# A planned schedule with one v fetch per batch, traced landing times, and the last strided outputs transposed by transfer

## The chip, the cores and the metric

The kernel runs on one core of a Trainium2 chip. The core has a matrix engine (TensorE, "PE"), a vector engine (VectorE, "DVE"), a scalar engine (ScalarE, "ACT"), a general engine (GpSimd, "POOL"), a queue engine that only issues transfers (SyncE, "SP"), and 16 transfer engines that carry what GpSimd and SyncE issue. TensorE reads from the on-chip memory SBUF and writes into eight banks of PSUM, which ScalarE and VectorE empty. The metric is the time of one execution on the device in microseconds (us), the median of several runs.

## The reference

Attention over 8 batches, 8 heads, 576 positions of 64 numbers each, and then a two-layer feed-forward part over the 4608 tokens. The first four heads see the last 32 positions ("local"); the last four see every 32nd position back ("strided").

```python
scores = scale * np.matmul(q, k.transpose(0, 1, 3, 2))
mask_local = (rel >= 0) & (rel < 32)
mask_strided = (rel >= 0) & (pos[None, :] % 32 == pos[:, None] % 32)
scores = np.where(masks, scores, -1e9)          # local for heads 0-3, strided for 4-7
attn = softmax(scores)
x = np.matmul(attn, v)                          # to (4608 tokens, 512)
h = x @ w_in                                    # 512 -> 2048
r = np.maximum(h, 0.0)
g = s * (r * r) + b
out = g @ w_out                                 # 2048 -> 512
```

The inputs are 32-bit, and so is the output; the kernel works in 16-bit floats, and GpSimd's transfers convert on the way in.

## The kernel before

The kernel is one long program without loops on the chip. While it is built, a planner with a clock of its own decides in which order the instructions of each engine stand. Nothing on the chip waits for that clock: the chip runs each engine's instructions in the order given, and each waits for its own inputs. A planned duration or landing time therefore moves instructions and costs nothing itself.

The planner knows three engines ("A", "V", "P" for ScalarE, VectorE, GpSimd) and three kinds of transfers issued by SyncE: "D", transposes within SBUF, "X", stores of x to a scratch in DRAM, and "Y", transposes back from there. LAT is the time from the end of the issue to the landing, in ns.

```python
class Plan:
    LAT = {"A": 70.0, "V": 70.0, "P": 70.0, "D": 12000.0, "X": 7000.0, "Y": 12000.0}
    ...
            eng = min(p[1], key=lambda e: max(self.free[e], r) + p[1][e])
            end = max(self.free[eng], r, self.t - self.SLACK) + p[1][eng]
            ...
                self.done[k] = end + (6000.0 if soon else p[4] or self.LAT[eng])
```

The loads of v. The local half is put in SBUF as bands of 96 positions, 32 partitions up, with a column of ones beside each 64 numbers; the strided half comes whole for batches 0 to 3 ("vs", then cast) and head by head later.

```python
    def v_band(b, h):
        return v[b, h].rearrange("(t p) d -> p t d", p=LQ)          # 96 rows of 6 x 64
    ...
    def load_vl(b):
        vl = v_loc[b % NV]
        for h in range(4):
            nc.gpsimd.dma_start(out=vl[LPAD:128, h, :, 0:D], in_=v_band(b, h))

    def load_vs(b):
        vs = v_str[b % NV]
        for h in range(4):
            nc.gpsimd.dma_start(out=vs[:, h, :, 0:D],
                                in_=v[b, 4 + h].rearrange("(p j) d -> p j d", j=ST))
```

The planned landings of what GpSimd fetches: one ring in which each transfer comes after the one before.

```python
    def landing(cost):
        nonlocal ring
        ring = max(ring, plan.t + 2000.0) + cost
        return ring + (6000.0 if plan.t > 60000.0 else 600.0)

    def weights_in(eng):                # after batch 0's loads
        ...
        load_w_in()                     # three parts: 512, 512, 1024 columns
        ring = 15300.0
        for keys, cost in ([0], 2700), ([1], 2500), ([2, 3], 5000): ...

    def second(eng):                    # batch 1, then w_out in four parts
        fetch_qk(1)
        load_vl(1)
        plan.done["raw", "vl", 1] = landing(3200)
        ...
        early_v(1)
        weights_out(range(4))           # landing(2400 if c < 3 else 3000)
```

The attention output x of one pair of heads becomes the transposed input xT of the feed-forward part in one of two ways: by TensorE against the identity, through PSUM, and a copy; or by transfer. The strided outputs by transfer go out to DRAM and come back transposed.

```python
        x_by_dma = b >= 2 if loc else XS_DMA <= b < B - 1      # XS_DMA = 4
        ...
        def xtrans(j, group):           # one transpose on TensorE (line 662)
            ...
                nc.tensor.matmul(out=st["px"][:, nq * j:nq * j + nq], lhsT=st["x"][:, j, :],
                                 rhs=ident[0:nq, 0:nq], is_transpose=True)
        def x_out(eng):                 # line 685
            nc.sync.dma_start(out=x_dram[2 * (b % 2) + mm].rearrange("(p j) d -> p j d", j=nt),
                              in_=st["x"])
        def x_in(eng):                  # line 689
            nc.sync.dma_start_transpose(out=x_slot(m, b), in_=x_dram[2 * (b % 2) + mm])
```

TensorE's main lines are: 429 and 437 the transposes of q and k, 557 the scores, 614 attention times v, 662 the transposes of x, 907 the first feed-forward matmul, in nine blocks of 512 tokens, 965 and 875 the second, and 1201 matmuls without use in the first 21 us.

```python
        # 907: needs the four xT pieces of the block's tokens and a part of w_in
        needs.append(("w_in", ft // 4))
        # 965: needs a piece of g and a quarter of w_out
        s = Step(f, 216, needs=[("g", T, ft), ("w_out", ft // 4)], ...)
```

## Time and profile before

| | before |
|---|---|
| time, median of 3 runs | 305.05 us (304.64 to 305.45) |
| span of the profiled execution | 304.4 us |
| TensorE, instructions of matmul kind | 2674 |
| GpSimd busy | 99.3 us, 33% |
| transfers: GpSimd's queue, SyncE's queue | 18.08 MB in 57232 packets; 18.78 MB in 43562 |
| v band fetches, each 72 KB | 28, 8.5 us from issue to landing (median) |
| ScalarE waiting for the first feed-forward matmul | 69.9 us, in 74 waits |

A line of the waits reads: engine, tile and line that waited, what ended the wait, the total in us, the number of waits, the longest. In a timeline the columns are the start in us, the length, the engine, the line, the operation with what it writes and reads, the number of like instructions merged, and in brackets the idle time of the engine before it with what ended it. Matmuls overlap: the recorded length of one is longer than the distance from its start to the next start.

### The profile page before, as it was taken

The page shows a single profiled execution, that of the slowest core. Times are in us where ns is not written, and L with a number is a line of the kernel's source. Part 1 is how long each engine was busy: PE and PEld are TensorE (multiplying, and loading weights), DVE is VectorE, ACT ScalarE, POOL GpSimd, SP SyncE. Part 2 cuts the span into 40 slices and gives each one's busy share as a digit, 9 for nine tenths or more (in the row PEclk, how much of TensorE's full clock was granted, in tenths as well). Part 3 has the DMA queues.
Part 4 walks back from the last instruction along what each step waited for, and adds up shares of the span by engine and source line. Part 5 has one row for each costly group of instructions (what it writes and reads, how often), then busy time and mean ns, then how long its engine had stood idle before and what let it go on. Part 6 is the DMA issues. An engine that isn't in the chain of part 4 may idle for free.

```text
span 304.4 us, 6800 instructions
## 1 busy us (share of the span) xinstructions
PE 296.4 (97%) x2674; PEld 205.8 (68%) x2674; DVE 216.6 (71%) x474; ACT 183.9 (60%) x330; POOL 99.3 (33%) x146
## 2 busy tenths in 40 slices
PE   8998999999999999999999999999999999999995
PEld 3764655666555568767567776778888666766784
DVE  6665897698966688737997698777765366737563
ACT  2966963898747677478585946695725445445300
POOL 8771753930961095029502961200000000000000
PEclk9999999999999999999999999999999999999999
DMA  8999999999999699999999999944010200300123
GB/s 136 183 201 202 137 213 190 179 198 149 83 160 165 98 100 149 132 186 147 142 153 172 142 160 159 155 105 131 14 37 34 72 34 0 106 0 2 69 82 126
DMA packets 100826, 37.29 MB, mean 122 GB/s; under 512 B 80907, under 2 KB 97803, under 8 KB 100795
## 3 DMA queue, kind: packets, MB, share of 16 engines
q0 software_dynamic: 57232, 18.08, 60.1%
q1 hardware_dynamic: 43562, 18.78, 33.3%
q8 instruction: 21, 0.34, 0.5%
q14 instruction: 11, 0.08, 0.1%
HBM read 36.86 MB, written 10.32 MB: 155 GB/s over the span
## 4 chain that ended last, share of the span: by engine, by line
PE 83%; DMA 8%; DVE 3%; POOL 3%; issue 1%; ACT 1%; POOLq 0%
PE ps_f L907 36%; PE ps_f L875 20%; PE ps_f L965 12%; DMA kl<-in_k_dram 5%; PE ps_s L557 3%; PE ps_a L614 3%; DMA vs<-in_v_dram 2%; PE ps_s L875 2%; DMA xT<-x_dram 1%; PE ps_t L875 1%; PE ps_s L965 1%; PE ps_t L614 1%; PE ps_t L662 1%; PE ps_t L437 1%; PE ps_f L437 1%
## 5 line engine op out<-in xcount | busy, mean ns | idle before, releaser
L907 PE MATMUL ps_f<-xT,w_in_sb 128*128 128x512 f16 (+4 forms) x696 | 148.1, 340 | 0.0
L934 ACT ACTIVATE u<-ps_f 128x512 f16<-128x512 f32 x137 | 80.8, 595 | 72.6 <-PE ps_f L907 69.9
L907 PEld LDWEIGHTS <-w_in_sb 128*128 128x128 f16 x704 | 71.7, 113 | 33.1 <-DMA w_in_sb<-in_moe_w_in_dram 0.5
L875 PEld LDWEIGHTS <-gT 128*128 128x128 f16 x512 | 49.0, 98 | 12.5 <-issue 0.4
L965 PE MATMUL ps_f<-w_out_sb,gT 128*128 128x512 f16 x176 | 47.6, 379 | 0.0
L875 PE MATMUL ps_f<-w_out_sb,gT 128*128 128x256 f16 x312 | 44.2, 273 | 0.3 <-DVE o L806 0.3
L944 DVE TENSOR_TENSOR gT<-u 128x1024 f16<-128x1024 f16 x46 | 32.1, 697 | 15.1 <-ACT u L934 14.4
L942 ACT ACTIVATE gT<-u 128x1024 f16<-128x1024 f16 x26 | 27.5, 1057 | 0.7
L640 DVE TENSOR_TENSOR x_nat<-ps_a,rec 72x256 f16<-72x256 f32 (+1 forms) x55 | 25.3, 459 | 0.9
L316 POOL DMA_DIRECT2D v_loc<-in_v_dram x28 | 20.7, 759 | 14.3 <-DMA w_in_sb<-in_moe_w_in_dram 6.0
L965 PEld LDWEIGHTS <-gT 128*128 128x128 f16 x192 | 17.0, 98 | 11.1
L575 ACT ACTIVATE p_str<-ps_s 72x432 f16<-72x432 f32 (+1 forms) x45 | 20.1, 481 | 4.7 <-PE ps_s L557 4.6
L575 ACT ACTIVATE p_loc<-ps_s 128x384 f16<-128x384 f32 x46 | 20.8, 494 | 2.2 <-PE ps_s L557 1.8
L614 PEld LDWEIGHTS <-p_str 72*128 72x128 f16 x256 | 15.3, 98 | 7.3 <-issue 0.4
L747 DVE TENSOR_TENSOR gT<-gT 128x1024 f16<-128x1024 f16 x28 | 18.5, 683 | 1.4 <-ACT gT L942 1.3
L875 PE MATMUL ps_f<-w_mix,gT 128*128 128x256 f16 x144 | 19.3, 273 | 0.0
L875 PEld LDWEIGHTS <-S 128*128 128x128 f16 x160 | 15.5, 98 | 3.7
L629 DVE RECIPROCAL rec<-ps_a 72x4 f32<-72x4 f32 (+1 forms) x55 | 9.7, 177 | 11.2 <-PE ps_a L614 11.0
L321 POOL DMA_DIRECT2D v_str<-in_v_dram x16 | 13.0, 816 | 9.6 <-PE ps_f L907 5.6
L583 DVE TENSOR_TENSOR p_loc<-p_loc,masks 128x1152 f16<-128x1152 f16 x14 | 10.5, 750 | 7.6 <-ACT p_loc L575 7.4
L875 PE MATMUL ps_f<-w_mix,S 128*128 128x256 f16 x96 | 13.4, 273 | 0.0
L976 DVE SCALAR_TENSOR_TENSOR o<-ps_f,s_sb,bcs 128x512 f32<-128x512 f32 x11 | 8.2, 749 | 6.4 <-PE ps_f L965 6.2
(162 smaller groups left out, 413.2 us busy)
## 6 DMA issues: line engine op xcount, KB each, us to landing
out_dram<-o SPq DMA_DIRECT2D x34, 256.0 KB, 3.4
w_out_sb<-in_moe_w_out_dram POOLq DMA_DIRECT2D x4, 512.0 KB, 9.4
v_loc<-in_v_dram POOLq DMA_DIRECT2D x28, 72.0 KB, 8.5
qs<-in_q_dram POOLq DMA_DIRECT2D x6, 288.0 KB, 6.6
ks<-in_k_dram POOLq DMA_DIRECT2D x6, 288.0 KB, 8.0
ql<-in_q_dram POOLq DMA_DIRECT2D x5, 288.0 KB, 9.7
kl<-in_k_dram POOLq DMA_DIRECT2D x16, 72.0 KB, 3.8
v_str<-in_v_dram POOLq DMA_DIRECT2D x16, 72.0 KB, 9.9
```

Of the source, the lines that this page charges most:

```text
L316: nc.gpsimd.dma_start(out=vl[LPAD:128, h, :, 0:D], in_=v_band(b, h))
L321: nc.gpsimd.dma_start(out=vs[:, h, :, 0:D], in_=v[b, 4 + h].rearrange("(p j) d -> p j d", j=ST))
L575: nc.scalar.activation(out=st["pw", g][0:nk, 0:2 * n * nq], in_=st["s", g][0:nk, 0:2 * n * nq], func=AF.Exp, scale=scale)
L614: nc.tensor.matmul(out=st["a"][:, j % per, :], lhsT=st["pw", g][0:nk, i * nq:i * nq + WIDE], rhs=vt[0:nk, 2 * mm + e, j, :])
L640: nc.vector.tensor_tensor(out=st["x"][:, j0:j0 + per, 64 * e:64 * e + 64], in0=st["pa", e, j][0:nq, 0:per, 0:D], in1=st["rec", e, j][0:nq, ...
L747: nc.vector.tensor_tensor(out=at(out), in0=at(x), in1=at(y), op=op)
L875: nc.tensor.matmul(out=gts[name, T, t][:, 0] if halves else gts[name, T][:, t], lhsT=lhs(k, t), rhs=rhs(k), start=fresh and k == 0 and (ha ...
L907: nc.tensor.matmul(out=gts["h", T, ft][:, lo:hi], lhsT=w_in_sb[min(ft // 4, 2)][:, ct].rearrange("p (c x l) -> p c l x", x=128, l=4)[:, ma ...
L934: nc.scalar.activation(out=u, in_=gts["h", T, ft], func=AF.Relu)
L942: nc.scalar.activation(out=g, in_=u, func=AF.Square)
L944: nc.vector.tensor_tensor(out=g, in0=u, in1=u, op=ALU.mult)
L965: nc.tensor.matmul(out=gts[id_], lhsT=gts[T][:, ft, ts * 128:(ts + 1) * 128], rhs=w_out_sb[:, ft, cols], start=(ft == 0), stop=(ft == NFT ...
```

## The change

Three things are changed. The local band of v of a batch is fetched in one transfer of 96 partitions by 24 runs of 64 numbers, instead of four of 6 runs. The planner's landing times are set to what a trace showed: of the transposes and stores (LAT), of the ring's tail after 60 us of the planner's clock, and of each early fetch. And the strided outputs of the last batch go by transfer like those of batches 4 to 6, instead of over TensorE. The aim is an order in which no engine stands before an input that has not landed, and less work on TensorE.

```diff
--- before.py
+++ after.py
@@ -21,7 +21,7 @@
 
 
 
-    LAT = {"A": 70.0, "V": 70.0, "P": 70.0, "D": 12000.0, "X": 7000.0, "Y": 12000.0}
+    LAT = {"A": 70.0, "V": 70.0, "P": 70.0, "D": 10000.0, "X": 6500.0, "Y": 6000.0}
 
     SLACK = 800.0
     LATER = {"g": 1500.0, "S": 1500.0, "in": 2500.0, "w_mix": 2500.0}
@@ -311,9 +311,9 @@
             nc.gpsimd.dma_start(out=h4(dst)[r], in_=view_s(src, b)[r])
 
     def load_vl(b):
-        vl = v_loc[b % NV]
-        for h in range(4):
-            nc.gpsimd.dma_start(out=vl[LPAD:128, h, :, 0:D], in_=v_band(b, h))
+        nc.gpsimd.dma_start(
+            out=v_loc[b % NV].rearrange("p h t d -> p (h t) d")[LPAD:128, :, 0:D],
+            in_=v.rearrange("b h (t p) d -> b p (h t) d", p=LQ)[b, :, 0:4 * LT])
 
     def load_vs(b):
         vs = v_str[b % NV]
@@ -475,7 +475,7 @@
 
         k_by_dma = b >= (KB_DMA if loc else 3)
         q_by_dma = b >= (QB_DMA if loc else QS_DMA)
-        x_by_dma = b >= 2 if loc else XS_DMA <= b < B - 1
+        x_by_dma = b >= 2 if loc else XS_DMA <= b
 
         def k_dma(eng):
             if loc:
@@ -1024,7 +1024,7 @@
         nonlocal ring
         ring = max(ring, plan.t + 2000.0) + cost
 
-        return ring + (6000.0 if plan.t > 60000.0 else 600.0)
+        return ring + (3500.0 if plan.t > 60000.0 else 600.0)
 
     def both(name, b):
         return [("in", name, b, mm) for mm in range(2)]
@@ -1041,13 +1041,13 @@
                 arrive(both(name + "l", b), landing(4600))
                 continue
             if b < HEAD_T:
-                arrive(both(name + "l", b), landing(1500))
+                arrive(both(name + "l", b), landing(2400 if name == "q" else 2600))
                 continue
-            plan.done["raw", name, b] = landing(1700 if b > 1 else 1450)
+            plan.done["raw", name, b] = landing(1700 if b > 1 else 2400 if name == "q" else 2500)
             for mm in range(2):
                 pair_post(b, name, mm, ("raw", name, b))
         for name in ("qs", "ks"):
-            arrive(both(name, b), landing(2000 if b > 1 else 1750))
+            arrive(both(name, b), landing(2000 if b > 1 else 1200))
 
     def fetch_v(b):
         load_vl(b)
@@ -1064,7 +1064,7 @@
 
         loaded[b, "vs"] = inp.tile([SQ, NS], FP16, tag="vs", name="vs")
         load_s(loaded[b, "vs"], v, b)
-        plan.done["raw", "v", False, b] = landing(1800)
+        plan.done["raw", "v", False, b] = landing(1800 if b > 1 else 1300)
         for mm in range(2):
             cast_v(b, False, mm, ("raw", "v", False, b))
 
@@ -1113,13 +1113,13 @@
 
         fetch_qk(1)
         load_vl(1)
-        plan.done["raw", "vl", 1] = landing(3200)
+        plan.done["raw", "vl", 1] = landing(2000)
         for mm in range(2):
             rows_before(1, mm, ("raw", "vl", 1))
         early_v(1)
         weights_out(range(4))
 
-    plan.post(both("vl", 0) + both("vs", 0) + [("w",)], {"P": 14000.0}, second, [("free",)])
+    plan.post(both("vl", 0) + both("vs", 0) + [("w",)], {"P": 12500.0}, second, [("free",)])
 
     att = []
     left = {}
@@ -1146,7 +1146,7 @@
                         {"P": 2900.0 + (2200.0 if b + 2 >= QB_DMA else 0.0)},
                         lambda eng, b=b: fetch_qk(b + 2), [("fetch", b + 2)])
                 last_av.after = when_all("av", b, lambda b=b: plan.post(
-                    [("fetch", b + 2)] + both("vs", b), {"P": 3600.0}, lambda eng: fetch_v(b + 2),
+                    [("fetch", b + 2)] + both("vs", b), {"P": 3600.0 if b >= 2 else 1500.0}, lambda eng: fetch_v(b + 2),
                     [("fetch_v", b + 2)]))
 
     f1, f2 = [], []
```

## The prediction

> **What bounds the kernel now.** I read the page's busy times and slices first, then the list of what TensorE waited for, then TensorE's and GpSimd's timelines over the one stretch where those waits lie. Busy times and slices (40 equal slices of 7.6 us, tenths):
>
> ```profile
> PE 296.4 (97%) x2674; PEld 205.8 (68%) x2674; DVE 216.6 (71%) x474; ACT 183.9 (60%) x330; POOL 99.3 (33%) x146
> ...
> PE   8998999999999999999999999999999999999995
> ...
> DMA  8999999999999699999999999944010200300123
> ```
>
> TensorE is full from the fourth slice to the last. The transfer engines are full for the first 26 slices, but TensorE hardly notices after the start. All of its waits (total us, times, longest):
>
> ```profile
> PE ps_t L429 <- DMA ql<-in_q_dram: 1.4, 1, 1.4
> ...
> PE ps_t L429 <- DMA kl<-in_k_dram: 0.6, 1, 0.6
> ...
> PE ps_f L875 <- DVE o L806: 0.3, 1, 0.3
> PE ps_a L614 <- DVE x_nat L640: 0.2, 1, 0.2
> ```
>
> (The three lines left out are in the first 19 us, which the change does not touch.) Where the first two lie, TensorE's timeline: start, length, line, operands, idle before it.
>
> ```profile
> 23.00 4.05 PE L907 MATMUL ps_f<-xT,w_in_sb 128*128 128x512 f16 x18
> 28.49 0.45 PE L429 MATMUL ps_t<-ident,ql 96*64 96x96 f16 x12 [1.44 <-DMA ql<-in_q_dram]
> 28.77 0.42 PE L429 MATMUL ps_f<-ident,ql 96*64 96x96 f16 x12
> 29.12 1.49 PE L907 MATMUL ps_f<-xT,w_in_sb 128*128 128x512 f16 x6
> 31.23 0.45 PE L429 MATMUL ps_t<-ident,kl 96*64 96x96 f16 x12 [0.62 <-DMA kl<-in_k_dram]
> ```
>
> Eighteen 512-column matmuls in 4.05 us, the last recorded as 0.38, are 216 ns from start to start. Then TensorE stands still for batch 1's q and k, with other work at hand: the third part of w_in had landed by 26.9, as GpSimd's timeline of the same stretch shows.
>
> ```profile
> 22.06 0.75 POOL L316 DMA_DIRECT2D v_loc<-in_v_dram  x1 [1.96 <-DMA w_in_sb<-in_moe_w_in_dram]
> 26.89 0.72 POOL L316 DMA_DIRECT2D v_loc<-in_v_dram  x1 [4.08 <-DMA w_in_sb<-in_moe_w_in_dram]
> 28.73 0.73 POOL L316 DMA_DIRECT2D v_loc<-in_v_dram  x1 [1.11 <-DMA ql<-in_q_dram]
> 31.47 0.72 POOL L316 DMA_DIRECT2D v_loc<-in_v_dram  x1 [2.01 <-DMA kl<-in_k_dram]
> 32.31 1.18 POOL L311 DMA_DIRECT2D vs<-in_v_dram  x2
> 33.63 2.15 POOL L334 DMA_DIRECT2D w_out_sb<-in_moe_w_out_dram  x4
> ```
>
> Each v band waits for the transfer issued eight places before it: GpSimd's transfers in this trace count on eight semaphores in turn. So the four bands go out over 10 us, the last at 31.5, and the queue nearly runs dry behind them. The transfer view of 33 to 36 us, in slices of 75 ns:
>
> ```profile
> GB/s 96 111 111 121 120 126 108 84 82 72 36 50 65 65 92 77 38 34 10 38 79 79 118 145 68 123 150 177 191 177 164 218 191 164 178 177 191 150 191 260
> ```
>
> From 33.5 to 35 it moves some 60 GB/s where the band ran at 120 just before and w_out runs at 180 after.
>
> [...] matmuls recorded as 379 ns start every 216. [...] the bands take 0.75 us on GpSimd and land 3.9 to 14.9 us after issue. [...] w_out's 128 rows take 554 ns to issue, a band's 576 rows 752.
>
> **Part 1, v in one transfer.** Seven batches by three fewer issues are 21 off GpSimd. From the two issue times, (752-554)/(576-128) = 0.44 ns per row; one issue of 2304 rows is then about 1.5 us, an estimate, against 4 x 0.75 = 3.0. That is 7 x 1.5 = 10 us off an engine that is 33% busy: worth nothing by itself. Rows and bytes stay the same, so a full queue gains nothing either. What it can gain is the hole: the whole band would go out at 22.1, the strided v at 26.9 and 28.7 and w_out from about 31.3, each again behind the eighth before it. 1.5 us at 60 instead of 120 GB/s is about 0.8 us, so w_out's first quarter, which by the trace's completion events landed at 40.2, should land near 39.4.
>
> **Part 2, the order of early work.** The built instruction order shows the same TensorE sequence up to the last of the 18 matmuls, then five 512-column matmuls before the q transposes where there were none, and eight between those and the k transposes where there were six.
> - Before q: 5 x 0.216 = 1.08 us of the gap filled. Gap from the 18th matmul's slot end (26.9) to 28.49 was 1.6; 0.5 stays.
> - Before k: 2 x 0.216 = 0.43 filled; of 0.8 [...] 0.4 stays. Together 1.5 us gained by 31.3.
> - Given back 1: the new order puts the first scores right behind qs, at 31.23 plus two sets of 12 k transposes at 22 ns, one matmul and eight at 32 ns = 32.2. In the old trace the k copy to SBUF ended at 32.35. About 0.2 lost.
> - Given back 2: summing start-to-start spacings (216 ns for 512 columns, 82 for 192, 63 for 144, 33 for 65, 32 for 72) along the new order, the first w_out matmul falls at 38.8, with the 0.2 at 39.0, where the old one ran at 40.8. It then waits for w_out until 39.4: 0.4 lost. If part 1 moves no landing it waits until 40.2 and loses 1.2, which is most of the gain. So the two parts hang together.
> - The wait before an attention matmul at 41.8, 0.4 of lost start time: in the new order the multiply that frees its bank stands further ahead. Counted as 0.4 gained.
>
> Part 2 nets 1.5 - 0.2 - 0.4 + 0.4 = 1.3 us.
>
> **Part 3, the last strided outputs.** Sixteen transposes of 72 columns leave TensorE, 104 to 88 of this kind:
>
> ```profile
> L662 PE MATMUL ps_t<-ident,x_nat 72*128 72x72 f16 x72 | 5.1, 196 | 0.0
> ...
> xT<-x_dram SPq DMA_TRANSPOSE x6, 3.3
> ```
>
> Recorded 196 ns each, they start every 32, so 16 x 32 ns = 0.5 us, and it counts, since TensorE is the bound there (215 to 219 us). Two copies also leave PSUM. The way round through DRAM costs two stores and two transposes, 3.3 us to land, with the last strided values ready by 219 and block 7, which reads them, starting at 237.0. It is hidden.
>
> **Part 4, shorter planned latencies.** They run nothing faster; they let consumers stand earlier. From block 2 on the attention steps stand some 8 to 10 us earlier in TensorE's order against the feed-forward blocks. That removes perhaps half of the single later loss (0.47 us before 177.4, behind a full VectorE): 0.25. The danger is an order that trusts a landing too much. Traced issue-to-landing of the in-SBUF transposes is 2.6 to 10.6 us, so at most 9.3 after the 1.3 us of issue, under the 10 now planned; of the DRAM ones 2.7 to 4.8, under 6. I charge 0.3 for a new wait.
>
> Sum: 1.3 + 0.5 + 0.25 - 0.3 = 1.75; the full sum of spacings along both orders from 39.1 and 43.1 on differs by 2.3 at the end, before the charge. I take 2.1: 305.05 - 2.1 = 302.9.
>
> **Rivals.** (a) The w_out landing takes the wait's place and nothing is kept of part 2: 0.5 to 1.0 gained in all, 304.3. For it: the queue is full, first in, first out, and the bytes are the same. Against it: the hole above. (b) The new order stalls in the middle, where three engines were in balance; the earlier attention crowds ScalarE and VectorE (more squares go to ScalarE, 26 to 31): 304 to 307. For it: landings of 10.6 us in crowded stretches; against: none of these waits showed before, and planned latencies were far above the traced ones. (c) The one large issue blocks GpSimd or the ring, w_out comes later, 305 to 306. For: 2304 rows at once was never run here; against: some 1,850 rows were already outstanding at 22 us (w_in 512, ql and kl 384 each, qs and ks 288 each).
>
> **Range and chances.** TensorE has about 3.5 us to give at most: the waits after 19 us (1.6, 0.8, 0.4, 0.47) and the transposes, so below 301.5 is not reachable, and the 2% line at 298.9 is out of reach. Slower by 2%, 311.2, would need new waits of 8 us. 8 in 10: 301.8 to 304.8. Chances 0.01 faster, 0.97 same, 0.02 slower.
>
> **What would show it.** Right: the waits for ql and kl near 0.5 and 0.4; w_out in flight by 34 us with no dip before it; the first L965 matmul near 39.4; block 7 about 2 us earlier; L662 at 88. Wrong: L965 waiting for w_out by over 1 us (part 1), or any single TensorE wait above 0.5 us after 60 us (part 4).

## The result and the profile after

| | before | after |
|---|---|---|
| time, median of 4 runs each, on one chip | 304.85 us (304.5 to 305.45) | 313.95 us (312.82 to 318.16) |
| ratio | | 1.0293, 95% interval 1.0258 to 1.0328 |
| span of the profiled execution | 304.4 us | 315.6 us |
| TensorE, instructions of matmul kind | 2674 | 2658 |
| ScalarE and VectorE waiting with a copy for a v band | none | 10.3 us in 3 waits and 8.4 us in 2 |

The change costs 2.9%. The prediction was 302.9, with 304.8 as the upper end of its range. The profiled execution of after is the longest of its executions (318.16), so its losses are larger than those of the median. The other executions on record span 310.4 to 312.1 us at mean clocks of 0.993 to 1.000, so by an estimate from the lowest of these clocks, (1 - 0.993) x 311.3, at most 2.2 us of theirs are due to the clock; none of them has a trace.

The page of after, busy times and slices (40 slices of 7.9 us, tenths; the third row is the granted clock of TensorE):

```profile
PE 299.9 (95%) x2658; PEld 206.9 (66%) x2658; DVE 213.8 (68%) x472; ACT 188.6 (60%) x334; POOL 85.8 (27%) x121
...
PE   7999989999999999999959994999999999999995
PEclk9999999999999999999979999899999999999999
DMA  8999999997999799999999999923500200200223
```

TensorE has two holes that it did not have before, in slices 21 and 25 (a 5 and a 4). The clock row shows less than nine tenths in slice 21 itself and in slice 26. What TensorE waited for, in the list of its waits:

```profile
PE ps_f L907 <- ACT u L934: 7.8, 2, 4.1
...
PE ps_a L429 <- DMA kl<-in_k_dram: 0.5, 1, 0.5
```

The first line is nearly everything: two waits, 7.8 us, by the first feed-forward matmul for a free PSUM bank, which ScalarE (line 934, the eviction to u) had not emptied. The kl wait is in the first batch's loads at the very start (7.5 us); batch 1's ql and kl waits, which the change was aimed at, are gone. TensorE's timeline at both places:

```profile
155.86 0.82 PE L875 MATMUL ps_f<-w_out_sb,gT 128*128 128x256 f16 x6
156.52 1.03 PE L907 MATMUL ps_f<-xT,w_in_sb 128*128 128x512 f16 x4
161.30 1.02 PE L907 MATMUL ps_f<-xT,w_in_sb 128*128 128x512 f16 x4 [3.75 <-ACT u L934]
...
191.23 0.82 PE L875 MATMUL ps_f<-w_out_sb,gT 128*128 128x256 f16 x6
196.14 1.53 PE L907 MATMUL ps_f<-xT,w_in_sb 128*128 128x512 f16 x4 [4.09 <-ACT u L934]
```

Why was ScalarE late? Its own timeline around the two places:

```profile
155.39 0.58 ACT L934 ACTIVATE u<-ps_f 128x512 f16<-128x512 f32 x1
160.04 0.73 ACT L338 COPY v_loc<-v_loc 32x640 f16<-32x640 f16 x1 [4.07 <-DMA v_loc<-in_v_dram]
160.67 1.05 ACT L934 ACTIVATE u<-ps_f 128x512 f16<-128x512 f32 x2
...
194.88 0.73 ACT L338 COPY v_loc<-v_loc 32x640 f16<-32x640 f16 x1 [5.16 <-DMA v_loc<-in_v_dram]
195.51 1.05 ACT L934 ACTIVATE u<-ps_f 128x512 f16<-128x512 f32 x2
```

A small copy (line 338: it puts the last 32 rows of one part of the v band under the next part) stood in ScalarE's order at a place where the band had not landed. ScalarE stood idle before it for 4.07 and 5.16 us, and the evictions behind it start only at 160.67 and 195.51. The waits of TensorE, 3.75 and 4.09 us, are put down to these evictions and end at 161.30 and 196.14. The copy itself takes 0.7 us and TensorE does not need it at that moment. VectorE stood before the twin of this copy at the same time, for 2.97 and 5.43 us until 160.04 and 194.88, so neither of the two engines that empty the banks did so meanwhile. The two bands are those of batches 6 and 7, counted from 0: GpSimd fetches seven, for batches 1 to 7, and these are the last two. (The quoted expectations call them those of batches 5 and 6.) The chain that ended last runs the same way (start, length, what):

```profile
141.69 18.33 DMA v_loc<-in_v_dram
160.04 0.73 ACT v_loc L338
160.76 0.49 ACT u L934
161.30 1.04 PE ps_f L907 x4
...
178.00 16.86 DMA v_loc<-in_v_dram
```

The bands took 18.3 and 16.9 us from issue to landing. What the two holes cost, from the table of busy times by stretch, for after (each hole, and the stretch behind it in which the trace has the clock at half; stretch, sum, then busy time and instructions of PE, weight loads, VectorE, ScalarE, GpSimd, then the mean granted clock, the transfer share, GB/s):

```profile
157.00:161.30 4.30, 0.55 (x4) 0.18 (x3) 1.30 (x4) 1.26 (x3) 0.00 (x0) 1.00 1.61 175
162.39:165.80 3.41, 3.41 (x19) 2.47 (x17) 1.17 (x3) 1.66 (x4) 0.00 (x0) 0.50 1.40 163
191.50:196.20 4.70, 0.61 (x7) 0.42 (x5) 1.02 (x2) 1.32 (x3) 0.00 (x0) 1.00 1.51 167
196.52:199.93 3.41, 3.41 (x10) 1.36 (x9) 2.49 (x4) 0.73 (x3) 0.00 (x0) 0.50 1.65 163
```

Start time lost in the holes, counted from where the next matmul would have started: 3.9 + 4.3 = 8.2 us. Lost to the lower clock, an estimate from the two stretches at 0.50: 2 x 3.41 x (1 - 0.50) = 3.4. Together 11.6 us, against a span longer by 315.6 - 304.4 = 11.2. So the loss of the profiled execution is all here, and whatever else the change moved comes to about -0.4.

The blocks of the first feed-forward layer say the same: the last matmul of block 0 starts 1.3 us earlier than before (39.15 against 40.41), that of block 4 6.8 us later (180.35 against 173.59), that of block 5 12.4 us later (216.28 against 203.92), and from the start of block 6 to the last matmul of block 8 after is 1.2 us shorter (74.29 against 75.51).

### The profile page after: what moved, and what is told of

Same layout as the page of the kernel before. It is cut to its first block, busy times and chain, and to the rows that moved or that the text cites. A ratio compares the mean times of both kernels' runs of the same rounds, so it can differ in the third digit from the quotient of the medians.

```text
span 315.6 us, 6716 instructions
## 1 busy us (share of the span) xinstructions
PE 299.9 (95%) x2658; PEld 206.9 (66%) x2658; DVE 213.8 (68%) x472; ACT 188.6 (60%) x334; POOL 85.8 (27%) x121
## 4 chain that ended last, share of the span: by engine, by line
PE 65%; DMA 21%; POOL 6%; issue 3%; DVE 2%; ACT 1%; SPq 1%; POOLq 0%; DVEq 0%
PE ps_f L907 28%; PE ps_f L875 16%; DMA v_loc<-in_v_dram 11%; PE ps_f L965 9%; DMA vs<-in_v_dram 5%; DMA ql<-in_q_dram 3%; PE ps_s L557 3%; PE ps_a L614 2%; DMA kT<-ks 2%; POOL ql L293 2%; PE ps_s L875 2%; PE ps_t L875 1%; PE ps_s L965 1%; POOL kl L293 1%; PE ps_t L437 1%
## 5 line engine op out<-in xcount | busy, mean ns | idle before, releaser
L907 PE MATMUL ps_f<-xT,w_in_sb 128*128 128x512 f16 (+4 forms) x696 | 150.5, 343 | 7.8 <-ACT u L934 7.8
L907 PEld LDWEIGHTS <-w_in_sb 128*128 128x128 f16 x704 | 72.6, 114 | 41.8 <-issue 9.4
L875 PEld LDWEIGHTS <-gT 128*128 128x128 f16 x512 | 49.5, 99 | 12.7 <-issue 0.6
L965 PE MATMUL ps_f<-w_out_sb,gT 128*128 128x512 f16 x176 | 48.3, 379 | 0.2
L944 DVE TENSOR_TENSOR gT<-u 128x1024 f16<-128x1024 f16 x41 | 28.1, 685 | 19.4 <-ACT u L934 18.9
L942 ACT ACTIVATE gT<-u 128x1024 f16<-128x1024 f16 x31 | 32.8, 1057 | 1.5 <-DVE u L936 0.6
L965 PEld LDWEIGHTS <-gT 128*128 128x128 f16 x192 | 17.1, 98 | 12.2 <-issue 1.0
L747 DVE TENSOR_TENSOR gT<-gT 128x1024 f16<-128x1024 f16 x28 | 18.5, 682 | 2.0 <-ACT gT L942 1.8
L1036 POOL COPY gate<-kT 1x1 f16<-1x1 f16 x6 | 2.1, 354 | 47.7 <-DMA kT<-ks 47.7
L614 PEld LDWEIGHTS <-p_loc 128*128 128x128 f16 x192 | 9.3, 98 | 5.1 <-DVE p_loc L583 0.9
## 6 DMA issues: line engine op xcount, KB each, us to landing
ks<-in_k_dram POOLq DMA_DIRECT2D x6, 288.0 KB, 10.3
```

The source lines that it names most:

```text
L614: nc.tensor.matmul(out=st["a"][:, j % per, :], lhsT=st["pw", g][0:nk, i * nq:i * nq + WIDE], rhs=vt[0:nk, 2 * mm + e, j, :])
L747: nc.vector.tensor_tensor(out=at(out), in0=at(x), in1=at(y), op=op)
L875: nc.tensor.matmul(out=gts[name, T, t][:, 0] if halves else gts[name, T][:, t], lhsT=lhs(k, t), rhs=rhs(k), start=fresh and k == 0 and (ha ...
L907: nc.tensor.matmul(out=gts["h", T, ft][:, lo:hi], lhsT=w_in_sb[min(ft // 4, 2)][:, ct].rearrange("p (c x l) -> p c l x", x=128, l=4)[:, ma ...
L942: nc.scalar.activation(out=g, in_=u, func=AF.Square)
L944: nc.vector.tensor_tensor(out=g, in0=u, in1=u, op=ALU.mult)
```

## The experiments

All ratios below are against the kernel before, run beside it on the same chip, with 95% intervals. They leave out executions more than 1.5% above the kernel's fastest, which hides part of a loss that comes and goes: of the 20 executions of the tail alone (306.11 to 315.26 us) six are left out, and the median of all 20 is 1.0% above before, where its ratio says 0.65%. Waits of TensorE that are given without a line are lost start time, from where the next matmul would have started; a line's brackets hold the idle time, which is up to 0.4 us less. The names of theories are those in the quoted expectations. "Early" stands for the landings and issue times of batch 1 and of the early v fetch, "tail" for the ring's 6.0 or 3.5 us after 60 us, "LAT" for the line of latencies, "last x" for the last batch's strided outputs by transfer.

### Each part alone

**One v transfer, all else as before.** The order on TensorE, ScalarE and VectorE is that of before.

```diff
-        for h in range(4):
-            nc.gpsimd.dma_start(out=vl[LPAD:128, h, :, 0:D], in_=v_band(b, h))
+        nc.gpsimd.dma_start(
+            out=v_loc[b % NV].rearrange("p h t d -> p (h t) d")[LPAD:128, :, 0:D],
+            in_=v.rearrange("b h (t p) d -> b p (h t) d", p=LQ)[b, :, 0:4 * LT])
```

> The kernel before with only the v band fetched in one transfer; the order on TensorE, ScalarE, VectorE and SyncE is that of before, instruction for instruction. Theory A (a late landing and an early copy are both needed): the band lands some 16 to 18 us after its issue instead of 8 to 10, for batch 5 near 160.5, but the copies that read it stand at 161.4 in this order, so no wait above 1 us: 304.3 to 305.5 us. Rival B (the single transfer does it alone): ScalarE and VectorE wait for the band for 3 us or more in one or two batches: 308 us or more.

308.73 us (306.58 to 311.25), ratio 1.0088 (1.0059 to 1.0117). GpSimd's timeline of this kernel at batch 6's band

```profile
145.71 1.20 POOL L314 DMA_DIRECT2D v_loc<-in_v_dram  x1
```

and ScalarE's:

```profile
161.98 1.35 ACT L338 COPY v_loc<-v_loc 32x640 f16<-32x640 f16 x2
```

The band lands at 160.4, 14.7 us after its issue; in before the four went out at 142.6 to 144.8 and the last landed at 154.8, 12.2 us after the first issue. For batch 7 it is 14.9 against 10.4 us. The copies stand late enough not to wait (161.98), but the 6.6 us of room that before had are down to 1.6. The span of the profiled execution is 305.2 and holds no wait above 1 us after 60 us. Some of the loss lies outside the span: time minus span is 2.25 us here and 1.8 in before. The rest comes and goes between executions, which spread over 4.7 us: five of the ten have mean clocks of 0.989 to 0.994, and none of these has a trace. Neither theory holds as it stands: no wait, as A had it, but the time that B wanted. Why the single transfer costs 0.9% is not shown.

**The early landings alone, the tail alone, LAT alone, last x alone.**

```diff
# early_alone: the hunks of fetch_qk, fetch_v, early_v, second and the last one
-            plan.done["raw", name, b] = landing(1700 if b > 1 else 1450)
+            plan.done["raw", name, b] = landing(1700 if b > 1 else 2400 if name == "q" else 2500)
# ...
# tail_alone
-        return ring + (6000.0 if plan.t > 60000.0 else 600.0)
+        return ring + (3500.0 if plan.t > 60000.0 else 600.0)
# lat_alone
-    LAT = {"A": 70.0, "V": 70.0, "P": 70.0, "D": 12000.0, "X": 7000.0, "Y": 12000.0}
+    LAT = {"A": 70.0, "V": 70.0, "P": 70.0, "D": 10000.0, "X": 6500.0, "Y": 6000.0}
# last_x_alone
-        x_by_dma = b >= 2 if loc else XS_DMA <= b < B - 1
+        x_by_dma = b >= 2 if loc else XS_DMA <= b
```

> The kernel before with only the landings of the first two batches, of w_in's and w_out's time and the two early planned issue costs changed; v in four transfers, tail and latencies of before. Theory E (the early part is sound; what costs is that attention was moved ahead from batch 2 on): the waits for ql and kl fall as in the changed kernel, a wait of up to 1.2 us for w_out appears, nothing waits above 0.5 us after 60 us; 303.5 to 305 us. Rival F (the early order upsets the later one): 306 us or more.

305.86 us, ratio 0.9990 (0.9971 to 1.0009). The ql and kl waits are gone; in their place TensorE waits 0.91 us for w_out at 38.4, which lands at 39.3. In time nothing is gained, where 303.5 to 305 were expected (before had 305.84 beside it).

> The kernel before with only the planned tail of GpSimd's fetches at 3.5 us instead of 6.0; v in four transfers. Of 704 first-layer and the second-layer matmuls, 436 stand ahead of the first use of batch 5's v band, against 471 before and 427 in the changed kernel. Theory E: the tail alone moves attention ahead, SyncE's transposes fall over GpSimd's fetches, v and k land later than their consumers stand, and TensorE waits 1 to 4 us in batches 5 and 6: 308 to 313 us. Rival D (it takes the shorter latencies of SyncE's transposes as well): 304.5 to 306.5 us.

308.89 us, ratio 1.0065 (1.0036 to 1.0094). New waits of 2.65 us at 187.6, for a q piece that VectorE lays out, and 1.71 at 190.6. VectorE's timeline of this kernel shows what the q piece stood behind:

```profile
189.22 0.32 DVE L338 COPY v_loc<-v_loc 32x640 f16<-32x640 f16 x1 [3.52 <-DMA v_loc<-in_v_dram]
189.56 1.28 DVE L338 COPY qD_loc<-qTl 64x576 f16<-64x576 f16 x4
```

and TensorE's:

```profile
190.24 0.49 PE L557 MATMUL ps_s<-qD_loc,kT_alt 128*128 128x192 f16 x4 [2.48 <-DVE qD_loc L338]
```

So the short tail alone, with four v transfers, already puts copies of batch 7's band ahead of its landing (VectorE waits 6.4 us in two), and the same blocking passes on to TensorE. That band's last quarter lands at 189.1, 18.5 us after the first issue.

> The kernel before with only the planned latencies of SyncE's transposes and stores shortened (10.0, 6.5 and 6.0 us); v in four transfers, tail 6.0. 451 matmuls of the two layers stand ahead of batch 5's v band. Theory E: half of the shift of the changed kernel, so smaller waits: 305 to 308 us. Rival D: these latencies are the main cause: 309 us or more.

307.05 us, ratio 1.0036 (1.0011 to 1.0060). New waits after 60 us: 1.61 us at 196.7, for a transposed k piece, and 1.0 at 203.3, for a mask. The traced execution is the longest of the twenty (311.09).

> The kernel before with only the last batch's strided outputs transposed by transfer; all planned latencies and the four v transfers as before. Sixteen TensorE transposes fewer, 32 ns each from start to start: 0.5 us less, 305.2 to 305.5 beside a before of about 305.8. Rival H: the two stores and two transposes added between 200 and 215 us fall over other transfers and something waits: 306 us or more.

307.17 us, ratio 1.0036 (1.0014 to 1.0058): sixteen matmuls fewer, and slower. TensorE's timeline of this kernel:

```profile
237.90 1.47 PE L875 MATMUL ps_f<-w_out_sb,gT 128*128 128x256 f16 x12 [0.84 <-DVE Va L794]
239.20 1.89 PE L907 MATMUL ps_f<-xT,w_in_sb 128*128 128x512 f16 x8
```

Block 7 starts at 239.2 instead of 237.0. The planner believed that the transposed pieces come back 12 us after issue ("Y"), so it kept block 7 back and put second-layer matmuls there, which then waited for their banks. So the time is rival H's, by another cause.

None of the five parts alone has a ratio above 1.009, and the sum of their losses is 2.2%, less than the 2.9% of all together.

### Taking parts back out of after

**Four v transfers again, in after's order.**

```diff
-        nc.gpsimd.dma_start(out=v_loc[b % NV].rearrange(...)[LPAD:128, :, 0:D], ...)
+        for h in range(4):
+            nc.gpsimd.dma_start(out=vl[LPAD:128, h, :, 0:D], in_=v_band(b, h))
```

> The changed kernel with only the v band fetched in four transfers again; the order on TensorE, ScalarE, VectorE and SyncE is that of the changed kernel. Theory A: each last quarter lands 10 to 12 us after its issue, near 154 for batch 5, before its copies at about 156; no wait of TensorE above 1 us after 60 us, 302 to 304 us. Rival C (the earlier order fills the queues so that v comes late however it is fetched): the quarters of batch 5 land at 158 or later and the waits of about 4 us stay: 309 us or more.

312.78 us, ratio 1.0239 (1.0211 to 1.0268). Most of the loss stays, so it is not the single transfer that makes it. ScalarE's timeline of this kernel at batch 6's copies

```profile
155.72 0.73 ACT L338 COPY v_loc<-v_loc 32x640 f16<-32x640 f16 x1
```

VectorE's:

```profile
159.75 0.32 DVE L338 COPY v_loc<-v_loc 32x640 f16<-32x640 f16 x1 [3.02 <-DMA v_loc<-in_v_dram]
```

and TensorE's:

```profile
160.91 0.49 PE L875 MATMUL ps_f<-w_out_sb,gT 128*128 128x256 f16 x3 [2.78 <-DVE Va L794]
```

With quarters each copy waits for its own two. ScalarE's finds them landed; VectorE's stands 3.0 us before the last one, at 159.7. The four had gone out at 141.1 to 143.3, 1.5 us earlier than in before, and landed up to 4.9 us later: 152.7 to 159.7 against 151.1 to 154.8. So the order alone, with the same transfers, delays the landing. The v copies are not all of it: of TensorE's late waits here as much goes to transposed k pieces that land late, 1.7 us at 166.7 and 1.5 at 198.7:

```profile
168.41 0.57 PE L557 MATMUL ps_s<-qD_str,kT 128*72 128x144 f16 x6 [1.56 <-DMA kT<-ks]
```

**The old tail in after.**

```diff
-        return ring + (3500.0 if plan.t > 60000.0 else 600.0)
+        return ring + (6000.0 if plan.t > 60000.0 else 600.0)
```

> The changed kernel with only the planned tail of GpSimd's fetches after 60 us at 6.0 us again instead of 3.5. Theory A: the copies of the v band's rows stand 2.5 us or more later, the band still lands 15 to 18 us after issue; the waits of ScalarE for the band fall from 10.3 us in all to under 3, 302.5 to 305 us. Rival B (the single transfer is late whatever is planned): waits of 3 us or more stay, 308 us or more. Rival D (the shorter latencies of SyncE's transposes are the cause, not the tail): waits stay as they are, 312 to 314 us.

308.72 us, ratio 1.0098 (1.0060 to 1.0137). One planning number gives two thirds of the loss back; the 302.5 to 305 that theory A expected are missed by what is left, about the cost of the single transfer. VectorE's timeline of this kernel at batch 6:

```profile
165.54 0.57 DVE L338 COPY v_loc<-v_loc 32x640 f16<-32x640 f16 x2
```

The band lands at 163.1, 17 us after its issue at 146.1, as slowly as in after; but the copies stand at 165.5 and do not wait. No wait after 60 us is above 0.73.

**The copies of v alone later in after.** Only the planned landing of the band is raised by 6 us; q and k keep after's numbers.

```diff
-            plan.done["raw", "vl", b] = landing(4600)
+            plan.done["raw", "vl", b] = landing(4600) + 6000.0
```

> The changed kernel with only the planned landing of the v band 6 us later from batch 2 on, so that the copies of its rows stand later on ScalarE and VectorE. Theory A (these copies block the engines in order, and with them the evictions that TensorE waits for): no wait for the band above 1 us, 302 to 304.5 us. Rival C (v is late for the attention itself, or the queues are clogged): TensorE waits as long at another place, 309 us or more.

311.04 us, ratio 1.0183 (1.0138 to 1.0229), where theory A expected 302 to 304.5. The v waits are gone, but others have come up. From TensorE's timeline of this kernel:

```profile
195.77 0.37 PE L614 MATMUL ps_a<-v_loc,p_loc 128*128 128x65 f16 x6 [0.56 <-DVE p_loc L583]
...
198.21 0.57 PE L557 MATMUL ps_s<-qD_str,kT 128*72 128x144 f16 x6 [1.45 <-DMA kT<-ks]
```

Now the scores wait for transposed k pieces (their weight loads 2.7 us in 2 waits), and the attention matmuls for the masks. Moving the copies of v back thus gives 1.1 of the 2.9 per cent; in what stays, TensorE waits for other landings that the same tail makes the planner expect early. That these waits are the whole rest is not shown.

**Old LAT in after.**

```diff
-    LAT = {"A": 70.0, "V": 70.0, "P": 70.0, "D": 10000.0, "X": 6500.0, "Y": 6000.0}
+    LAT = {"A": 70.0, "V": 70.0, "P": 70.0, "D": 12000.0, "X": 7000.0, "Y": 12000.0}
```

> The changed kernel with only the latencies of SyncE's transposes and stores as before; tail 3.5, v in one transfer. 435 matmuls of the two layers stand ahead of batch 5's v band, against 427 in the changed kernel, 463 with only the tail restored, 471 before. Theory E (the further ahead attention stands, the longer the waits): between the 308.7 of the kernel with only the tail restored and the 314 of the changed one, 310 to 313 us. Rival D (these latencies are the main cause): 308 us or less.

320.00 us (316.58 to 320.73), ratio 1.0441 (1.0405 to 1.0477). The expectation was missed: with longer planned latencies it is the slowest kernel of all. It has the same two waits as after (3.85 at 157.9 and 4.49 at 192.0), and a clock row that is lower behind them:

```profile
PE   8999989999999999999969994999999999999995
PEclk9999999999999999999969997899999999999999
```

Behind each wait this trace has the clock at half for 6.83 us, twice as long as in after (160.61 to 167.44 and 194.74 to 201.57; the mean clock is 0.55 from 162 to 168 and 0.67 from 192 to 200), so by the same estimate up to 6.8 us are lost to it instead of 3.4 (for the first 1.1 and 1.7 us of the two TensorE still stood). The mean clocks of its six executions, 0.979 to 0.989, amount to 3.5 to 6.7 us lost, against 0 to 2.2 in the untraced ones of after. So by this estimate the clock can account for most of what it loses beyond after, 1.5% or about 4.5 us. Why its clock stays low for longer is not shown.

**Both numbers back, one v transfer; and both parts without any of the planned latencies.**

```diff
# late_plan_one_v: after, with tail 6000.0 and the old LAT
# early_and_last_x: before, with the early landings and last x (four v transfers)
```

> The changed kernel with both the planned tail and the latencies of SyncE's transposes as before; so the kernel above with v in one transfer, and the same order of TensorE, ScalarE, VectorE and SyncE as that one. Theory E: no more than the cost of the single transfer is left, about 2.7 us as in the run of that part alone: 307 to 308.5 us, no wait of 4 us. Rival B (the single transfer is the main cause): 310 us or more.

310.49 us, ratio 1.0154 (1.0120 to 1.0188); waits of 1.80 us at 197.3 and 1.00 at 239.8. The 307 to 308.5 expected are missed; the time is in rival B's range.

> The kernel before with the two parts kept that did no harm: the early landings and the last strided outputs by transfer. Four v transfers, tail 6.0, latencies of before; 471 matmuls of the two layers stand ahead of batch 5's v band, as before. Theory E: the early part gives 0.3 and the transposes 0.5 us; 304.5 to 305.3 beside a before of about 305.8, no TensorE wait above 0.5 us after 60 us. Rival: the gains do not add, 305.5 or more.

306.83 us, ratio 1.0032 (1.0013 to 1.0050); waits of 1.50 us for w_out at 39.0 (landed at 40.4) and 1.01 at 237.5. Here too the gain expected (304.5 to 305.3) did not come. The two kernels have the same order and differ in the v transfers alone: 1.2%.

**Four v transfers with the old tail, or with the old LAT.**

```diff
# four_v_tail_back: after, four v transfers, tail 6000.0
# four_v_lat_back: after, four v transfers, the old LAT (tail 3500.0)
```

> The changed kernel with v in four transfers and the tail at 6.0 us; the shorter latencies of SyncE's transposes, the early landings and the last strided outputs by transfer stay. Theory K (without the shortened tail nothing large is lost; the transfer and the latencies only make it worse): 0.998 to 1.004 of before, no wait above 1 us after 60 us. Rival D (the shorter latencies do it alone): 1.010 or more.

306.84 us, ratio 1.0026 (1.0005 to 1.0048). No late wait, as theory K expected; w_out is waited for 1.97 us at 39.3, since it landed at 41.3.

> The changed kernel with v in four transfers and the latencies of SyncE's transposes as before; the tail stays at 3.5 us. Theory K: the shortened tail costs by itself as in the run of that part alone and the four transfers land soon enough: 1.005 to 1.015 of before, against 1.044 with one transfer. Rival (the tail alone is enough for the whole loss): 1.025 or more.

313.96 us, ratio 1.0231 (1.0184 to 1.0278). The theory called K wanted 1.005 to 1.015, that is, tail and one transfer needed together; it falls. Its rival wanted 1.025 or more, which lies within the interval. With the early order and last x, the tail alone is enough for most of the loss. TensorE's waits in this kernel, the same kind as in after:

```profile
PE ps_f L907 <- ACT u L934: 6.8, 2, 4.7
```

With these, three of the parts are tried in all combinations, each with the early landings and last x. The rows and columns were not all run beside each other, so differences of 0.3% say little:

| | tail 6.0, old LAT | tail 6.0, new LAT | tail 3.5, old LAT | tail 3.5, new LAT |
|---|---|---|---|---|
| four v transfers | 1.0032 | 1.0026 | 1.0231 | 1.0239 |
| one v transfer | 1.0154 | 1.0098 | 1.0441 | 1.0293 (after) |

The mean of the right half less that of the left is +2.2%; one transfer instead of four is +1.15%; the new LAT is -0.5%, all of it from the kernels with one transfer. Every kernel of this study that is over 2% slower has the short tail, and none without it is over 1.6%.

### Why the fetches land later

The four quarters of the same bytes landed up to 4.9 us later in after's order than in before's. SyncE's timeline while batch 6's band is on its way (stores of the output left out), in before (band in flight from 142.6 to 154.8):

```profile
143.15 1.72 SPq L693 DMA_TRANSPOSE xT<-x_nat  x1
...
146.92 2.01 SPq L693 DMA_TRANSPOSE xT<-x_nat  x1
...
150.78 3.71 SPq L508 DMA_TRANSPOSE qTl<-ql  x2
```

and in after (band in flight from 141.7 to 160.0):

```profile
143.74 0.58 SPq L685 DMA_DIRECT2D x_dram<-x_nat  x1
144.63 4.21 SPq L693 DMA_TRANSPOSE xT<-x_nat  x2
...
149.53 0.45 SPq L685 DMA_DIRECT2D x_dram<-x_nat  x1
150.09 5.70 SPq L489 DMA_TRANSPOSE kT_loc<-kl  x2
155.89 3.78 SPq L516 DMA_TRANSPOSE qT<-qs  x2
```

Two stores of x, both kT_loc and two qT transposes have moved into the band's flight; in before it holds, besides the lines shown, one store of x right at its end. A count of the transfer records in steps of 1 us from 100 to 206 us gives about 40 us in before, and about 60 in after, in which GpSimd's fetches and SyncE's transfers are both moving. In those steps of after the fetches move about 50 GB/s, against about 127 in the steps in which they are alone (56 and 126 in before). So the fetches were slower in both orders while SyncE's transfers moved, and after has more such steps. Two runs test whether SyncE's work is the cause, one by taking part of it away and one by changing it.

**Without the moves of x for batches 4 to 7.** The order is after's. The kernel leaves out 8 transposes within SBUF, 8 stores and 8 transposes back from DRAM, so x does not reach the feed-forward part for those batches; every other instruction is there.

```diff
         def x_out(eng):
+            if b >= 4:
+                return
         def x_in(eng):
+            if b >= 4:
+                return
         def x_dma(eng):
+            if b >= 4:
+                return
```

> The changed kernel without the transfers that carry the attention outputs x of batches 4 to 7 to their transposed place (8 transposes within SBUF, 8 stores and 8 transposes by way of DRAM are left out; the first layer reads what earlier batches left there, so the time alone counts). All other instructions and their order are those of the changed kernel. Theory E (transposes and fetches in flight together slow each other): v of batches 5 and 6 lands at least 3 us sooner after its issue than the 18.3 and 16.9 of the changed kernel, and the two waits of about 4 us fall below 2: 303 to 308 us. Rival G (the fetch is slow by itself, by its many short rows or one large issue): landings within 1 us of the changed kernel's and 311 us or more.

306.85 us, ratio 0.9997 (0.9967 to 1.0027). The whole loss is gone. Batch 6's band lands at 155.4, 15.2 us after its issue, and batch 7's at 183.8, 12.7 after (18.3 and 16.9 in after). TensorE has no wait above 0.25 us after 60 us, and its slices show no hole:

```profile
PE   8989989999999999999999999999999999999995
```

The landings gain only 3 to 4 us, but that is the length of the waits. SyncE's other transposes come sooner too without the moves (the median for kT is 3.2 us, 6.6 in after), so the run does not tell what the v bands alone are worth.

**Plain copies in place of the transposes of x.** The same places in the order, with all of the bytes by way of DRAM and three quarters of them within SBUF, but untransposed, so x stands wrongly laid out in the feed-forward part of batches 4 to 7. The theory called M held that any traffic of SyncE delays the fetches; its rival, that it is the transposes as such.

```diff
-            nc.sync.dma_start_transpose(out=x_slot(m, b), in_=x_dram[...])
+            nc.sync.dma_start(out=x_slot(m, b), in_=x_dram[...].rearrange("s d -> (s d)").rearrange("(p x) -> p x", p=128))
# and for the transposes of x within SBUF a plain copy to 96 of the 128 partitions
```

> The changed kernel with the 16 transposes that carry the attention outputs of batches 4 to 7 replaced by plain copies to the same place (from SBUF three quarters of the bytes, by way of DRAM all of them), so that x arrives in a wrong order and the time alone counts; everything else and every order as in the changed kernel. Theory L (it is transposes in flight that slow the fetches): v of batches 5 and 6 lands 3 us or more sooner than 18.3 and 16.9 us after its issue, as without these transfers at all (15.2 and 12.7), and the time is 1.000 to 1.010 of before. Rival M (any traffic of SyncE's does it): landings within 1.5 us of the changed kernel's and 1.020 or more.

313.23 us, ratio 1.0227 (1.0190 to 1.0264). Batch 6's band still takes 18.3 us and TensorE waits 2.63 us at 158.8; batch 7's takes 12.9 and nothing waits for it. The time speaks for the traffic more than for the transposing. With one band for and one against, more than that can't be said.

### A version without the losses

Last x with the planned landing that belongs to it, the early landings, four v transfers, tail and LAT as before.

```diff
 # before, with the early landings and last x
-   plan.post([("xd", id_)] + x_free(b), {"Y": 1300.0}, x_in, [("xT", b, m)])
+   plan.post([("xd", id_)] + x_free(b), {"Y": 1300.0}, x_in, [("xT", b, m)],
+             6000.0 if b == B - 1 else None)
```

> The kernel before with the early landings and the last strided outputs by transfer, and for the last batch alone a planned landing of 6.0 us, instead of 12.0, for the transpose from DRAM. Theory J (the 1.0 us wait at 237 us comes from block 7 being planned for a landing that is long past): that wait is gone, 1 us less than with the same kernel without it, 0.995 to 0.999 of before. Rival H (the added transfers themselves disturb): 1.002 or more.

305.94 us, ratio 1.0005 (0.9983 to 1.0028). The wait at 237 is gone, so the 12 us were its cause, and after 60 us nothing waits above 0.25; the gain of 0.1 to 0.5% that theory J promised is not seen. What stays is 0.83 us lost for w_out at 39.3, 0.7 in the list of its waits:

```profile
PE ps_f L966 <- DMA w_out_sb<-in_moe_w_out_dram: 0.7, 1, 0.7
```

It has the lowest ratio of those that hold last x and do all of the work, and can't be told from the kernel before. No version here beats that one.

## Why the prediction was wrong

**The step that failed** is Part 4, "I charge 0.3 for a new wait". In the profiled execution it was 8.2 us of waits and 3.4 us of lower clock. The danger was named there, "an order that trusts a landing too much", and rival (b), "the new order stalls in the middle", was the right rival with too small an effect (up to 307). Three things were wrong in the working of that charge.

- It held the planned numbers against landings traced under the old order ("at most 9.3", "under the 10 now planned"). In the new order the same transfers land later: the median of the in-SBUF transposes of x goes from 4.5 to 7.5 us (of the 6 and 4 whose landing the traces show), of the k transposes from 2.9 to 6.6 (of 3 and 3), and four v bands in the new order have 9.3 instead of 8.5, with a worst of 16.4 instead of 14.9. SyncE's new planned numbers are still about kept (in-SBUF transposes of x at most 8.9 after the end of their issue, 10 planned; one from DRAM 6.1, 6.0 planned).
- It looked at SyncE's transposes only. What stalled was GpSimd's fetch of v, whose planned landing is shortened by the ring's tail, from 6.0 to 3.5. The prediction did not check the tail against the v landings, though it quotes their 14.9. What a shorter tail does by itself, the run of the tail alone shows.
- It counted a late landing as a wait of its one consumer. The consumer was a 0.7 us copy on ScalarE (0.3 on VectorE), and the evictions behind it started only at 160.67 and 195.51, so TensorE stood for 3.75 and 4.09 us for something it did not need yet. The page of before has no sign of that: the copies stood 6.6 us behind the landing there.

**Part 1**, that GpSimd's 10 us are worth nothing, held: 85.8 instead of 99.3 us busy, and no gain in time from it. The issue was 1.20 to 1.26 us against 1.5 estimated. The earlier landing of w_out that it promised did not come from the transfer: with one transfer alone w_out's first quarter goes out at 31.9, near the 31.3 worked out, and lands at 41.4, later than the 40.2 of before. (From 33.5 to 35 the view quoted for the hole has 75 GB/s on the mean, not 60, so by the same sum the hole was worth 0.6 us and not 0.8.) "Rows and bytes stay the same, so a full queue gains nothing either" was too kind: at the same order the one transfer lands 2.5 and 4.5 us later after the first issue than the last of the four, and costs 0.9%, in after's surroundings 0.5% (1.0293 against 1.0239).

**Part 2** came out nearly as worked out and was still worth nothing. TensorE's timeline of after, early stretch:

```profile
28.05 0.45 PE L429 MATMUL ps_t<-ident,ql 96*64 96x96 f16 x12
...
30.77 0.45 PE L429 MATMUL ps_t<-ident,kl 96*64 96x96 f16 x12
...
37.30 0.32 PE L614 MATMUL ps_a<-v_loc,p_loc 128*128 128x65 f16 x5 [0.28 <-ACT v_loc L338]
...
39.63 0.61 PE L965 MATMUL ps_f<-w_out_sb,gT 128*128 128x512 f16 x2
```

No idle time stands before ql and kl any more. The first w_out matmul starts at 39.63, where 39.4 was predicted, and block 0 ends 1.3 us earlier, where 1.3 was predicted. That w_out landed where it should is luck: with the early landings alone it lands at 39.3 without the single transfer, and three traces with the early order of before and four transfers (before, tail_alone, last_x_alone) have it at 40.2, 39.7 and 38.9, a spread larger than the effect. And new waits came: 0.7 us in two at 36.9 and 37.5 before matmuls that read v, 0.9 at 40.7 behind a mask. Block 1 starts at 57.01 against 56.98, so all of it is given back in one block; with the early landings alone it starts at 56.16. In time that run has 0.9990 (0.9971 to 1.0009), no gain that can be told from none. That is near rival (a): the next landing takes the wait's place. (Its "first in, first out" is what the trace of before shows: all 113 of GpSimd's transfers land in the order in which they were issued.)

**Part 3** has the right count (74 and 14 matmuls of line 662 in two tiles, 88) and left out that the order depends on the planned return: alone it costs 0.36%, with a planned landing of 6.0 us it costs nothing and gains nothing that shows. The expected 0.5 us is within its interval.

**The range.** "TensorE has about 3.5 us to give at most" limited the gain rightly, and the chance of a gain over 2% was rightly near nothing. That slower by 2% "would need new waits of 8 us" was the right size too; 0.02 for it was too low, since by the prediction's own Part 4 the attention steps moved 8 to 10 us forward in TensorE's order, and with them all that reads q, k and v. The sign that was to refute Part 4, "any single TensorE wait above 0.5 us after 60 us", is there twice.

**What stays open.** How large the tail's effect is depends on the rest of the order: alone it costs 0.65%, with the early landings and last x 2.0% (1.0231 against 1.0032). Where each landing falls against each copy was seen in the traces and not predicted. Nor is it settled why one transfer lands later than four of the same rows, which of SyncE's transfers delay the fetches most, or how the loss of after's shorter executions divides.

## What to carry to other kernels

A traced landing time did not hold here once the order had changed: with the same four transfers, batch 6's band landed up to 4.9 us later in after's order. If a plan that uses such a time moves work forward, leave room and check the moved plan's own trace. Ask of every instruction that waits for a transfer what stands behind it on its engine; a copy of 0.7 us ahead of PSUM evictions stopped the matrix engine here for 3.75 and 4.09 us. And merging transfers on an engine that was 33% busy gained nothing here, while the copies, which with quarters wait for two of them, wait for the whole band, which in before's order landed 2.5 and 4.5 us later after the first issue than the last quarter.

## What the runs showed of the hardware that was not expected

- One transfer of 2304 rows took 1.20 to 1.26 us to issue, against 4 x 0.75, but at the same order landed 2.5 to 4.5 us later after the first issue than the last of the four.
- Time minus span is 1.97 to 2.56 us in the profiled executions of the eight kernels with one v transfer, and 1.73 to 1.94 in those of the ten with four: a mean of about 0.4 us more that no engine's record shows.
- Behind the waits of 3.75 and 4.09 us in after TensorE's granted clock fell to half for 3.41 us each (162.39 to 165.80 and 196.52 to 199.93; by the estimate above 1.7 us of work lost each time), and in lat_back, from late in the waits of 3.85 and 4.49 us on, for 6.83 each. In four_v_lat_back, whose longest wait is 4.7 us, its mean is 0.79 from 192 to 200. With shorter waits it was mixed: behind idle times of 2.48 (tail_alone) and 2.47 us (plain_x_moves) the mean is 0.76 from 190 to 197 and 0.77 from 162 to 168, and behind one of 2.78 (four_v_again) it is 1.00 from 156 to 176. What decides between them, and what sets how long the clock stays at half, is not shown.
- GpSimd's fetches moved about 50 GB/s while SyncE's transfers were moving and about 127 alone in after (56 and 126 in before), and with plain copies in place of transposes one of two bands still took 18.3 us to land (the other 12.9, against 16.9 in after).
